# First expert stage of an attention, dense and routed-expert chain on one Trainium2 core: groups 2,3,3,3,3,2, an order planned with engine times, and part of the sums by accumulating transfers

## The chip, the core and the metric

The kernel runs on one core of one Trainium2 chip. Five engines work side by side, each through its own instruction list in order: PE (matrix multiplication), DVE and ACT (elementwise work), POOL and SP (here mainly issuers of transfers). Lists meet only at waits. The metric is device microseconds of the whole program.

## The reference

Four batches of 448 tokens pass through an attention, a dense layer pair and a routed layer pair:

```python
attn_out = _attn_ref(**attn_kwargs)          # (4, 12, 448, 64)
x = attn_out.transpose(0, 2, 1, 3).reshape(1792, 768)
h = x @ w_in                                 # (1792, 2048)
g = np.where(h > 0.0, h, np.exp(np.minimum(h, 0.0)) - 1.0)
x = g @ w_out                                # (1792, 768)
# then: argmax expert of x @ w_gate per token, relu(x @ w1[e]) @ w2[e], times the gate
```

The change touches the middle part, `h`, `g` and `g @ w_out`, called the first expert stage in its title. `w_in` and `w_out` arrive as doubles, read as pairs of 32-bit words, and are turned into floats on the chip ("decoding").

## The kernel before

All of the stage is in `moe1`. Products are made of two-part numbers: a value is split into a high part (an ACT copy to the matmul's type) and a low part (a DVE subtraction), in `hi_lo`. Each product takes three matmuls (high·high, high·low, low·high). Hidden units come in 16 blocks `f` of 128, tokens in four batches `b`. An "h unit" (`hmm`, L497) makes one `h[f, b]` in 18 matmuls of 448 columns. Its activation (`elu_act`, `elu_dve`) is three ACT steps (L511, L513, L514), two DVE steps (L522, L523), then the split (L470 on ACT, L471 on DVE). An "o unit" (`group_out`, L539) makes two of the six 128-row pieces `d` of `g @ w_out` for one batch, summed over the blocks of a group.

Batches 0 to 2 go first, group by group (`GROUPS`): all h units of a group, then its o units. Every piece of an o unit is taken from its PSUM bank by `group_evac`: the first group's is copied to `x2` (ACT L548, DVE L550), every later one is added to it by DVE (L552). Five banks (`acc0` to `acc4`) serve the pieces in turn; h units use two `h` banks and `acc5`. Blocks are decoded meanwhile (`Decoder.steps`): six steps, L138, L140 to L143 on DVE and L139 on ACT, then the row is split into `wi` or `wo` and stored to DRAM for the last batch. The blocks below `PRE` were decoded during the attention and are only loaded.

The order around it is written by a loop over units in `rest`. After each unit `background` spends a fixed budget on decoding and splitting (1.5 behind an h unit, 2.1 behind an o unit); a split is forced only when the unit that needs it is next. Two decoded rows at most wait (`len(held) < 2`, buffers `dec_p`). Loads and stores of rows stand on SP's list.

The last batch follows alone, block by block, with all weights loaded again. Between its units, and in the last group's o units, stand the routing steps of batches 0 to 2 (`route`).

The head of the stage overlaps the attention's end. `load_x` (L457) loads a batch's six tiles from DRAM into three `xraw` buffers, `split_x` splits them (L110, L112). The first two h units come between attention pieces; the tiles of batches 1 and 2 are split after the attention's last results (`p_av` L316, copied by L323, stored by L324).

## Time and profile before

| | us |
|---|---|
| median of 3 runs | 1301.95 |
| lowest, highest | 1298.39, 1317.82 |
| the profiled execution, its own time | 1304.9 |
| its span | 1303.1 |

In that execution PE is busy 1174.6 us (90%), DVE 793.1 (61%), ACT 661.6 (51%). The busy shares are means over stages with different limits, so the stretch of the stage is read by itself: when each phase begins, how many matmuls it holds, what PE waited for, and what clock was granted to it.

### The profile page before, as it was taken

The page shows a single profiled execution, that of the slowest core. Times are in us where ns is not written, and L with a number is a line of the kernel's source. Part 1 is how long each engine was busy: PE and PEld are TensorE (multiplying, and loading weights), DVE is VectorE, ACT ScalarE, POOL GpSimd, SP SyncE. Part 2 cuts the span into 40 slices and gives each one's busy share as a digit, 9 for nine tenths or more (in the row PEclk, how much of TensorE's full clock was granted, in tenths as well). Part 3 has the DMA queues.
Part 4 walks back from the last instruction along what each step waited for, and adds up shares of the span by engine and source line. Part 5 has one row for each costly group of instructions (what it writes and reads, how often), then busy time and mean ns, then how long its engine had stood idle before and what let it go on. Part 6 is the DMA issues. An engine that isn't in the chain of part 4 may idle for free.

```text
span 1303.1 us, 32292 instructions
## 1 busy us (share of the span) xinstructions
PE 1174.6 (90%) x13494; PEld 993.2 (76%) x13494; DVE 793.1 (61%) x1586; ACT 661.6 (51%) x1260; POOL 257.1 (20%) x424
## 2 busy tenths in 40 slices
PE   6889999899977996987969799888997999999996
PEld 2566566566666995977959698776897999999996
DVE  3777668667644746768577667344446555666663
ACT  3877778667754444152442433444444444455552
POOL 4756556556500000000000000000001101111110
PEclk7999999999988997998979899999997999999999
DMA  7787786776523422413223221333307747566661
GB/s 202 193 218 185 203 219 183 204 191 184 164 84 101 143 78 73 146 37 112 70 92 127 73 94 58 95 102 106 105 27 251 227 149 223 178 222 225 225 215 57
DMA packets 108991, 190.19 MB, mean 146 GB/s; under 512 B 44160, under 2 KB 68722, under 8 KB 108836
## 3 DMA queue, kind: packets, MB, share of 16 engines
q1 hardware_dynamic: 77284, 137.22, 33.6%
q0 software_dynamic: 31552, 50.82, 14.4%
q8 instruction: 108, 1.77, 0.6%
q14 instruction: 47, 0.39, 0.1%
HBM read 120.15 MB, written 30.09 MB: 115 GB/s over the span
## 4 chain that ended last, share of the span: by engine, by line
PE 72%; DVE 10%; ACT 9%; DMA 4%; issue 4%; POOL 0%; SPq 0%; POOLq 0%; ACTq 0%; DVEq 0%
PE p_o L539 12%; PE p_h L1106 11%; PE p_h L497 8%; PE p_z L1091 8%; PE p_post L281 6%; PE p_av L316 6%; PE p_pre L247 5%; PE p_qk L221 5%; PE acc L561 4%; PE p_y L1106 3%; DVE g L523 2%; DVE th L522 2%; DMA sp<-st 2%; ACT gh L470 2%; ACT th L513 2%
## 5 line engine op out<-in xcount | busy, mean ns | idle before, releaser
L238 POOL DMA_DIRECT2D sp<-st x360 | 207.8, 592 | 140.2 <-PE p_pre L247 72.2
L539 PE MATMUL p_o<-gh,woh 128*128 128x448 f32 x288 | 110.4, 383 | 43.0 <-ACT woh L470 34.2
L1053 POOL DMA_INDIRECT xg<-x2rows,tok x18 | 19.1, 1062 | 644.9 <-DMA x2rows<-rows 632.5
L258 ACT ACTIVATE pt<-p_pre,mx 128x448 f32<-128x448 f32 x180 | 112.5, 631 | 48.0 <-DVE mx L252 47.8
L281 PEld LDWEIGHTS p_post<-kp,pt 60*64 60x64 f32 (+1 forms) x5760 | 96.3, 134 | 50.4 <-ACT mt L291 31.3
L281 PE MATMUL p_post<-kp,pt 60*64 60x60 f32 (+1 forms) x5760 | 108.0, 220 | 15.1 <-issue 10.2
L252 DVE TENSOR_REDUCE mx<-p_pre 128x1 f32<-128x448 f32 x180 | 104.3, 619 | 28.1 <-PE p_pre L247 21.5
L291 ACT ACTIVATE mt<-p_post 128x960 f32<-128x960 f32 (+1 forms) x92 | 101.6, 1104 | 38.5 <-PE p_post L281 38.5
L497 PE MATMUL p_h<-xh,wih 128*128 128x448 f32 x288 | 109.8, 381 | 10.4 <-ACT wih L470 5.6
L522 DVE SCALAR_TENSOR_TENSOR th<-rm,th 128x448 f32<-128x448 f32 x64 | 40.0, 625 | 122.9 <-ACT rm L514 122.9
L1106 PE MATMUL p_h<-xgl,w1h 128*128 128x256 f32 (+1 forms) x384 | 110.0, 286 | 0.2 <-DVE xgl L1070 0.2
L1106 PE MATMUL p_h<-xgh,w1h 128*128 128x256 f32 (+1 forms) x384 | 110.1, 287 | 0.0
L221 PE MATMUL p_qk<-ks,qs 64*64 64x448 f32 x744 | 98.8, 561 | 12.6 <-issue 4.6
L1106 PE MATMUL p_h<-xgh,w1l 128*128 128x256 f32 (+1 forms) x384 | 109.8, 286 | 0.0
L539 PE MATMUL p_o<-gl,woh 128*128 128x448 f32 x288 | 108.8, 378 | 0.2 <-DVE gl L471 0.2
L539 PE MATMUL p_o<-gh,wol 128*128 128x448 f32 x288 | 108.8, 378 | 0.0
L497 PE MATMUL p_h<-xh,wil 128*128 128x448 f32 x288 | 108.1, 375 | 0.2 <-DVE wil L471 0.2
L497 PE MATMUL p_h<-xl,wih 128*128 128x448 f32 x288 | 107.7, 374 | 0.0
L316 PEld LDWEIGHTS p_av<-mt,vt 128*64 128x64 f32 x1536 | 78.0, 143 | 36.5 <-DVE kp L268 9.9
L247 PE MATMUL p_pre<-sp,kpre 60*64 60x448 f32 x720 | 101.3, 551 | 4.0 <-DMA sp<-st 4.0
L228 DVE COPY st<-p_qk 128x448 f32<-128x448 f32 x93 | 57.9, 623 | 73.0 <-PE p_qk L221 64.5
L539 PEld LDWEIGHTS p_o<-gh,woh 128*128 128x128 f32 x288 | 56.9, 197 | 51.0 <-ACT woh L470 35.3
(175 smaller groups left out, 2676.9 us busy)
## 6 DMA issues: line engine op xcount, KB each, us to landing
sp<-st POOLq DMA_DIRECT2D x352, 105.0 KB, 4.3
w1raw<-in_w_dram SPq DMA_DIRECT2D x64, 384.0 KB, 5.3
w2raw<-in_w_dram SPq DMA_DIRECT2D x48, 384.0 KB, 4.2
raw<-in_w_in_dram SPq DMA_DIRECT2D x13, 768.0 KB, 4.9
raw<-in_w_out_dram SPq DMA_DIRECT2D x13, 768.0 KB, 4.7
wtmp<-wscr SPq DMA_DIRECT2D x19, 384.0 KB, 3.2
wtmp<-oscr SPq DMA_DIRECT2D x19, 384.0 KB, 3.7
qs<-in_q_dram SPq DMA_DIRECT2D x32, 192.0 KB, 5.1
```

The lines of the kernel that those rows point to most:

```text
L221: mm(p[e][64 * a:64 * a + 64, :S], lhsT=qq[r, c:c + 64], rhs=kk[r], start=True, stop=True)
L238: nc.gpsimd.dma_start(t[64 * r:64 * r + 12 * T, c], st[cc][f:f + d * (T - 1) + 1:d])
L247: mm(ban[r][64 * c:64 * c + 64, :S], lhsT=kpre[x], rhs=t[x, c, :], start=True, stop=True)
L252: nc.vector.tensor_reduce(mxs[cc, g][:, r:r + 1], pre[cc, g][r][:, :S], AX.X, ALU.min)
L258: nc.scalar.activation(pt[cc, g][:, r], pre[cc, g][r][:, :S], AF.Exp, bias=mxs[cc, g][:, r:r + 1], scale=-1.0, accum_out=sms[cc, g][:, r:r ...
L281: mm(p[64 * (s % 2):64 * (s % 2) + 64, 2 * c + r, j * 12 * T:(j + 1) * 12 * T], lhsT=e[x, r, 64 * k0:64 * k0 + 64], rhs=kp[x, r].rearrange ...
L291: nc.scalar.activation(dst, src, AF.Copy)
L316: mm(p[64 * e:64 * e + 64, u, :n], lhsT=vt[cc // 4][:, j, h, :], rhs=mt[cc][:, j * H + h, :n], start=(j == 0), stop=(j == 3))
L497: mm(p[:, :S], lhsT=a[:, c], rhs=m, start=(i == 0), stop=(i == 17))
L539: mm(p[:, :S], lhsT=a[:, c], rhs=m, start=(k == 0), stop=(k == 3 * len(fs) - 1))
L1091: mm(zp[p][j, a][:, :384], lhsT=h2[h][:, i, c], rhs=w[:, a * 384:(a + 1) * 384], start=(i == 0 and m == 0), stop=(i == NFE - 1 and m == 2))
L1106: mm(q[:, :N], lhsT=a[:, kk, :], rhs=m[:, kk, :], start=(j == 0), stop=(j == len(seq) - 1))
```

## The change

Groups become 2,3,3,3,3,2 blocks; `PRE` stays 3. `background` now returns a planner: it keeps a running time for PE, ACT and DVE, adds a fixed cost for every step that is placed, and puts decoding and splitting steps one at a time into gaps of the plan (`fill_up`), between the steps of an activation too. The low part of an activation's split is placed late (`late`). `need` fixes the order of rows. Three decoded rows may wait instead of two. The sum of a piece goes to DVE as before, or to ACT (L572), which copies the bank to a tile `part` (four buffers, shared with `xraw`); POOL then issues a transfer that adds `part` to `x2` (L573). In the last group DVE takes all. The last group's units are interleaved (h of batches 0 and 1, o of 0, h of 2, o of 1 and 2), with up to two routing steps per o unit. At the head, batch 1 is loaded and split earlier and its first h unit stands ahead of the attention's last product. The activation writes in place (`th`, two buffers), and the rows of zeros that go to `x2rows` lie in the buffer of `rm`.

```diff
-GROUPS = [[0, 1, 2], [3, 4, 5], [6, 7, 8], [9, 10, 11], [12, 13], [14, 15]]
+GROUPS = [[0, 1], [2, 3, 4], [5, 6, 7], [8, 9, 10], [11, 12, 13], [14, 15]]
-PRE = len(GROUPS[0])
+PRE = 3
...
+    for b in (0, 1, None, 2, None, None):
+        if b is None:
+            units += [("o", len(GROUPS) - 1, outs, d) for d in range(0, KD, 2)]
+            outs += 1
+        else:
+            units += [("h", f, b) for f in GROUPS[-1]]
...
-        P["dec"] = Decoder(nc, sb, DM, 2, 1, 2)
+        P["dec"] = Decoder(nc, sb, DM, 2, 1, 3)
...
-            t = P["sb"].tile([128, S], F32, name="xraw", tag="xraw", bufs=3)
+            t = P["sb"].tile([128, S], F32, name="xraw", tag="xraw", bufs=4)
...
+        elif grouped:
+            to = wo[f] = pair(P["p1"], "wo", [128, DM], 4)
...
-    def group_evac(n, b, d):
+    def group_evac(n, b, d, dve):
...
+        elif dve:
+            nc.vector.tensor_tensor(x2[b][:, d, :], p, x2[b][:, d, :], ALU.add)
         else:
-            nc.vector.tensor_tensor(x2[b][:, d, :], p, x2[b][:, d, :], ALU.add)
+            t = P["sb"].tile([128, S], F32, name="part", tag="xraw", bufs=4)
+            nc.scalar.activation(t, p, AF.Copy)
+            nc.gpsimd.dma_start(x2[b][:, d, :], t, accum_op=ALU.add)
...
+        zrow = P["sb"].tile([128, S], F32, name="zrow", tag="rm")[:1]
...
+    need = []
+    for n, fs in enumerate(GROUPS):
+        need += [("in", f) for f in fs[:2] if n]
+        for i, f in enumerate(fs):
+            need += [("out", f)] + [("in", g) for g in fs[2 + i:3 + i]]
...
+        def put(e, ready, cost, fn):
+            T[e] = max(T[e], ready) + cost
+            fn()
+            return T[e] + .1
...
+                    raw[w, f] = P["dec"].load((w_in if w == "in" else w_out)[f]), max(T["dve"], T["act"]) + 6
...
+        DVE = {0: .6, 2: .6, 3: 1.0, 4: 1.0, 5: 1.0}
...
+                elif decs and decs[0] in raw and (len(started) < 3 or started[-3] in made):
+                    c.append((raw[decs[0]][1], .6, start))
...
+        def fill_up(e, until):
+            while True:
+                x = next_op(e)
+                if x is None or max(T[e], x[0]) + x[1] > until:
+                    return
+                x[2]()
...
             if v[0] == "o":
-                for d in (v[3], v[3] + 1):
-                    group_evac(v[1], v[2], d)
+                for i, d in enumerate((v[3], v[3] + 1)):
+                    at_end = end - (1 - i) * .61 * len(GROUPS[v[1]])
+                    fill_up("dve", at_end + .3)
+                    dve = n > last_n or T["dve"] < max(T["act"], at_end) + .1
+                    put("dve" if dve else "act", at_end, .65, lambda: group_evac(v[1], v[2], d, dve))
...
-                background(n, 1.5 if units[n][0] == "h" else 2.1)
...
+                relu, tanh, exp, w, sm, hi, lo = elu_steps(v[1:], place(i))
+                put("act", end, .6, relu)
+                put("act", end, .6, tanh)
+                e = put("act", end, .6, exp)
+                if late:
+                    put("dve", *late.pop())
+                fill_up("dve", e + .3)
+                fill_up("act", e + 1.1)
+                put("dve", e, .65, w)
+                e = put("dve", e, .65, sm)
+                late.append((put("act", e, .6, hi), .65, lo))
...
+    at(NSLOT + 1.5, 92, split_x, 1, range(3))
+    at(NSLOT + 1.5, 93, load_x, 1, range(3, 6))
+    at(NSLOT + 2, 94, split_x, 1, range(3, 6))
+    at(NSLOT + 2, 95, load_x, 2, range(4))
+    at(NSLOT + 2.2, 14, hmm, 0, 1, h_bank)
```

**First place: DVE, the step from a group's h units to its o units.** Before, at the end of the second group's h units (`wol` is the low part of a `w_out` row, `th`, `g` and `gl` belong to an activation, L138 to L143 decode, `x` is the sum):

```order
L141 SCALAR_TENSOR_TENSOR dec_m<-raw,dec_m 128x768
L142 SCALAR_TENSOR_TENSOR dec_p<-raw,dec_p 128x768
L143 SCALAR_TENSOR_TENSOR dec_p<-dec_m,dec_p 128x768
L471 TENSOR_TENSOR wol<-dec_p,woh 128x768
L522 SCALAR_TENSOR_TENSOR th<-rm,th 128x448
L523 SCALAR_TENSOR_TENSOR g<-p_o,th 128x448
L471 TENSOR_TENSOR gl<-g,gh 128x448
L138 TENSOR_SCALAR dec_p<-raw 128x768
L140 TENSOR_SCALAR dec_m<-raw 128x768
L141 SCALAR_TENSOR_TENSOR dec_m<-raw,dec_m 128x768
L552 TENSOR_TENSOR x_7732<-p_o,x_7732 128x448 x2
```

And in the changed kernel, at the same place of its second group (blocks 2, 3, 4):

```order
L143 SCALAR_TENSOR_TENSOR dec_p<-dec_m,dec_p 128x768
L536 SCALAR_TENSOR_TENSOR th<-rm,th 128x448
L537 SCALAR_TENSOR_TENSOR th<-p_h,th 128x448
L488 TENSOR_TENSOR gl<-th,gh 128x448
L488 TENSOR_TENSOR wol<-dec_p,woh 128x768
L536 SCALAR_TENSOR_TENSOR th<-rm,th 128x448
L537 SCALAR_TENSOR_TENSOR th<-p_h,th 128x448
L488 TENSOR_TENSOR gl<-th,gh 128x448
L138 TENSOR_SCALAR dec_p<-raw 128x768
```

The group's last `wol` has moved up: one activation (that of the ninth h unit) stands behind it before, two stand behind it now, and its decoding stands further ahead.

**Second place: ACT, the same group's o units.** Before (`part` doesn't exist, ACT takes no sums there):

```order
L470 ACTIVATE gh<-g 128x448
L139 ACTIVATE dec_p<-dec_p,ebias 128x768
L470 ACTIVATE wih<-dec_p 128x768
L139 ACTIVATE dec_p<-dec_p,ebias 128x768
L470 ACTIVATE wih<-dec_p 128x768
L139 ACTIVATE dec_p<-dec_p,ebias 128x768 x2
```

Now:

```order
L487 ACTIVATE gh<-th 128x448
L572 ACTIVATE part<-p_o 128x448 x5
L139 ACTIVATE dec_p<-dec_p,ebias 128x768
L487 ACTIVATE wih<-dec_p 128x768
L572 ACTIVATE part<-p_o 128x448 x2
L487 ACTIVATE wih<-dec_p 128x768
L139 ACTIVATE dec_p<-dec_p,ebias 128x768
L572 ACTIVATE part<-p_o 128x448 x2
L487 ACTIVATE woh<-dec_p 128x768
L139 ACTIVATE dec_p<-dec_p,ebias 128x768
L572 ACTIVATE part<-p_o 128x448 x3
```

Thirteen of the group's 18 pieces go through ACT and POOL (one more stands behind these rows), five in a row at its start; in the four groups after the first it is 13, 10, 13 and 10.

**Third place: SP, the loads at the head of the stage** (`xscr_61` and `xscr_62` hold batches 1 and 2, `xscr_63` takes the attention's last results). Before:

```order
L324 DMA xscr_63<-xc 128x2x88 x3
L478 DMA wtmp<-wscr_66 128x768
L478 DMA wtmp<-oscr_80 128x768
L457 DMA xraw<-xscr_61 128x448 x3
L457 DMA xraw<-xscr_62 128x448 x6
```

Now:

```order
L464 DMA xraw<-xscr_61 128x448 x6
L464 DMA xraw<-xscr_62 128x448 x4
L324 DMA xscr_63<-xc 128x2x88 x3
L464 DMA xraw<-xscr_62 128x448 x2
L495 DMA wtmp<-oscr_80 128x768
```

All of batch 1 and four tiles of batch 2 have moved ahead of the attention's last stores; two tiles of batch 2 still stand behind them.

## Rows read from the trace of the kernel before

**Rows 1.** The page's head.

```profile
span 1303.1 us, 32292 instructions
```

**Rows 2.** Stretches: length; busy PE, PEld, DVE, ACT, POOL (instructions); granted clock; DMA share, GB/s.

```profile
371.26:434.39 63.13, 50.29 (x355) 43.40 (x355) 28.75 (x50) 30.84 (x54) 0.00 (x0) 0.81 0.30 95
434.39:467.62 33.23, 33.10 (x164) 30.33 (x162) 24.38 (x39) 11.91 (x20) 0.00 (x0) 1.00 0.39 126
467.62:500.61 32.99, 32.99 (x163) 30.31 (x162) 17.90 (x27) 17.29 (x30) 0.00 (x0) 1.00 0.17 60
500.61:547.56 46.95, 35.55 (x163) 32.03 (x162) 36.49 (x55) 12.97 (x19) 0.00 (x0) 0.85 0.33 107
...
580.63:626.87 46.24, 34.82 (x164) 31.45 (x162) 36.39 (x55) 12.96 (x19) 0.00 (x0) 0.89 0.35 106
...
659.93:707.45 47.52, 36.13 (x164) 32.45 (x162) 36.30 (x55) 13.83 (x20) 0.00 (x0) 0.86 0.33 102
...
729.43:763.92 34.49, 25.61 (x109) 22.24 (x108) 27.87 (x44) 10.25 (x15) 0.00 (x0) 0.85 0.27 94
763.92:813.45 49.53, 48.95 (x256) 43.30 (x254) 29.76 (x64) 21.26 (x39) 0.00 (x0) 1.00 0.18 57
813.45:962.06 148.61, 132.86 (x665) 116.44 (x665) 65.96 (x140) 65.46 (x113) 0.00 (x0) 0.95 0.30 96
```

**Rows 3.** Who waited for whom on PE, 365 to 815 us.

```profile
PE p_o L539 <- ACT woh L470: 34.2, 3, 11.4
PE p_o L539 <- DVE x L552: 7.9, 2, 7.6
```

**Rows 4.** PE in order of time: start, us, line, operation, [idle before <-releaser].

```profile
386.29 6.68 PE L316 MATMUL p_av<-mt,vt 128*64 128x88 f32 x96 [3.47 <-ACT mt L291]
...
513.39 0.74 PE L539 MATMUL p_o<-gh,woh 128*128 128x448 f32 x1 [11.40 <-ACT woh L470]
...
515.30 0.57 PE L539 MATMUL p_o<-gl,woh 128*128 128x448 f32 x1
515.68 0.57 PE L539 MATMUL p_o<-gh,wol 128*128 128x448 f32 x1
```

**Rows 5.** DVE in order of time, ahead of the first long wait.

```profile
509.65 0.95 DVE L141 SCALAR_TENSOR_TENSOR dec_m<-raw,dec_m 128x768 f32<-128x768 uint32 x1
...
511.51 0.96 DVE L143 SCALAR_TENSOR_TENSOR dec_p<-dec_m,dec_p 128x768 f32<-128x768 f32 x1
```

**Rows 6.** Groups of instructions by shape, 434 to 764 us: busy, mean ns, idle before.

```profile
L552 DVE TENSOR_TENSOR x<-p_o,x 128x448 f32<-128x448 f32 x71 | 42.3, 619 | 9.4 <-PE p_o L539 9.2
L522 DVE SCALAR_TENSOR_TENSOR th<-rm,th 128x448 f32<-128x448 f32 x35 | 21.9, 624 | 49.5 <-ACT rm L514 49.5
L513 ACT ACTIVATE th<-rm 128x448 f32<-128x448 f32 x35 | 20.2, 578 | 1.1
L548 ACT ACTIVATE x<-p_o 128x448 f32<-128x448 f32 x9 | 4.6, 533 | 7.3 <-PE p_o L539 7.3
```

**Rows 7.** DMA queues: packets, MB, share of 16 engines; then issues: KB, us to landing.

```profile
q1 hardware_dynamic: 77284, 137.22, 33.6%
q0 software_dynamic: 31552, 50.82, 14.4%
...
sp<-st POOLq DMA_DIRECT2D x352, 105.0 KB, 4.3
...
raw<-in_w_in_dram SPq DMA_DIRECT2D x13, 768.0 KB, 4.9
...
xraw<-xscr SPq DMA_DIRECT2D x24, 224.0 KB, 3.0
```

**Rows 8.** ACT in order of time at the head.

```profile
386.14 1.50 ACT L110 ACTIVATE xh<-xraw 128x448 fp32r<-128x448 f32 x3
399.01 1.75 ACT L110 ACTIVATE xh<-xraw 128x448 fp32r<-128x448 f32 x3 [11.38 <-DMA xraw<-xscr]
```

**Rows 9.** Busy time by stretch, late in the program (columns as in group 2).

```profile
1193.00:1275.00 82.00, 82.00 (x607) 81.61 (x606) 51.35 (x77) 42.61 (x79) 14.69 (x16) 1.00 0.61 207
```

More of the change, by code (lines that the diff above doesn't have):

```diff
@@ L474, in scr, with load_row @@
         return (wscr if w == "in" else oscr)[f]
-    def load_row(w, f):
-        t = P["sb"].tile([128, 2 * DM], F32, name="wtmp", tag="raw", bufs=2)[:, :DM]
+    def load_row(w, f, t=None):
+        t = raw_tile()[:, :DM] if t is None else t
         nc.sync.dma_start(t, scr(w, f))
@@ L607, in row @@
             elif hf == 0:
-                T["row"] = P["sb"].tile([128, DM], F32, name="row", tag="dec_p", bufs=2)[:JC]
+                T["row"] = P["sb"].tile([128, DM], F32, name="row", tag="dec_p", bufs=3)[:JC]
             p = bank([JC, 3, 128], "tp")
@@ L814, in rest @@
         P["acc"] = pools.open("m_psacc", "right", PSUM)
-        need = sorted((where[w, f][0], w, f) for f in range(NF) for w in ("in", "out"))
-        need = [(w, f) for _, w, f in need if (w, f) not in (("in", 0), ("in", 1))]
-        loads, decs, splits = list(need), [k for k in need if k[1] >= PRE], list(need)
-        raw, cur, ready, held = {}, [], {k for k in need if k[1] < PRE}, set()
-        def free_after(w, f):
-            uses = where.get((w, f - (2 if w == "in" else 4)))
-            return uses[-1] if uses else -1
@@ L826, in load_next @@
-        def load_next():
-            if loads:
-                w, f = loads.pop(0)
-                if f < PRE:
-                    load_row(w, f)
-                else:
-                    raw[w, f] = P["dec"].load((w_in if w == "in" else w_out)[f])
-        def decode_step():
-            if not cur:
-                k = decs.pop(0)
-                held.add(k)
-                fns, dst = P["dec"].steps(raw.pop(k))
-                cur.extend([k, dst, fns])
-            k, dst, fns = cur
-            if len(fns) == 6:
-                for _ in range(3):
-                    fns.pop(0)()
-                return 1.1
-            fns.pop(0)()
-            if not fns:
-                rows32[k] = dst
-                ready.add(k)
-                cur.clear()
-                load_next()
-                nc.sync.dma_start(scr(*k), dst)
-            return .95
@@ L888, in weights @@
             load_pair(f + 3)
-        steps, banks, place = [], [0], {}
-        for n, u in enumerate(units):
-            if u[0] == "h":
-                g = [i for i, fs in enumerate(GROUPS) if u[1] in fs][0]
-                place[n] = sum(p[0] == "h" and p[1] in GROUPS[g] for p in units[:n])
-        ends = NU - KD // 2 * NG
-        load_next()
-        load_next()
-        for n in range(2, NU + 1):
-            if n == 2:
-                split_x(1, range(3))
-                load_x(1, range(3, 6))
-                split_x(1, range(3, 6))
+        steps, banks, late = [], [0], []
+        for n in range(3, NU + 1):
+            now = T["pe"]
             if n < NU:
@@ L905, in rest @@
                 if u[0] == "h":
+                    now = max(now, ready([("in", u[1])]))
                     hmm(u[1], u[2], h_bank if n % 3 < 2 else lambda: o_bank(5))
+                    T["pe"] = over[n] = now + 3.7
                 else:
+                    now = max(now, ready([("out", f) for f in GROUPS[u[1]]]))
                     for d in (u[3], u[3] + 1):
                         group_out(u[1], u[2], d, banks)
-            v = units[n - 1]
-            if v[0] == "o":
-                for d in (v[3], v[3] + 1):
-                    group_evac(v[1], v[2], d)
+                        if n >= last_n + 9 and steps:
+                            steps.pop(0)()
@@ new lines, in rest @@
+            if n < NU and late and units[n][0] == "o":
+                put("dve", *late.pop())
+            if n < NU:
+                for e in ("dve", "act", "dve"):
+                    fill_up(e, T["pe"] - (0 if e == "dve" else .5))
+            if n == 5:
+                fill()
+            if n == 20:
+                sel()
+            if 2 <= at_last < 2 + KD:
+                load_x(last_b, [at_last - 2])
+            if at_last == 6:
+                for f in range(2):
+                    load_row("in", f, P["sb"].tile([128, DM], F32, name="wtmp", tag="dec_p", bufs=3))
+                t = raw_tile()
+                for f in range(2):
+                    load_row("out", f, t[:, f * DM:(f + 1) * DM])
```

232 lines of the change are left out of this document (140 added, 92 removed).

## The prediction

> **What bounds it now.** I first read busy time by stretch, with bounds at the first matmul of each phase of the stage [rows 2]. The reader should see three kinds of stretch. An h phase of nine units, 162 matmuls, takes 32.99 us with PE busy throughout and the clock at 1.00, so 3.67 us a unit. The first group's o phase, also 162 matmuls, takes 33.23, or 0.205 us a matmul. The o phases of the next three groups hold the same 162 matmuls and take 46.95, 46.24 and 47.52, the fifth group's, of 108, takes 34.49, at granted clocks of 0.85 to 0.89. And the head, 63.13 us for nine h units, has a clock of 0.81.
>
> Then I read who PE waited for. In the o phases it was the high part of a `w_out` row, three times, 11.4 us at the longest, and once the sums on DVE, 7.6 of 7.9 us [rows 3]. The order of time shows the first of these: PE idles 11.40 us to 513.39, and afterwards matmuls start 0.38 us apart (515.30, 515.68) in place of 0.205, the lower of the two clock levels [rows 4]. On DVE the missing row's decoding steps end only with the one at 511.51, which lasts 0.96 [rows 5]. So PE sets the stage's time, and what it waits for is a decoding that DVE does late.
>
> DVE is late for two reasons. It is busy 17.90 of 32.99 us in an h phase but 36.49 in an o phase, which needs only 33.23 on PE [rows 2]: work is piled where there is no room. Over a whole group 54.4 of 66.2 would do.
>
> **Term 1, the stalls of groups two to five.** Against 33.23 (and 33.23·2/3 = 22.15 for two blocks) the four o phases lose 13.72 + 13.01 + 14.29 + 12.34 = 53.4 us [rows 2]; waits of 11.4, and 2 to 3 us of low clock behind each. In the changed order the group's last low part stands ahead of the last two activations of the h phase (first place), some 7 us before the first o unit, so the long wait has no source. The load moves too. Of each group's 18 sums ACT takes 13, 10, 13, 10, which frees DVE of 0.619 us each [rows 6]: 8.0 or 6.2 us, leaving 46 to 48 of 66.2. ACT gains 0.533 us a piece [rows 6], 6.9 us at most, on 17.29 + 12.97 = 30.3 [rows 2], so 37 of 66.2. Both fit with room, and the plan's fixed costs (0.6 for an activation step, 0.65 for DVE's) lie above the measured 0.578 and 0.624 [rows 6], so the order shouldn't drift late.
>
> In-order waits remain. ACT's decoding step stands behind five `part` copies, that is behind the sixth piece, 6·1.85 = 11 us into the o phase, and DVE's later decoding steps wait for it. This uses some 3 us of DVE's 18 us of slack per group. A late sum reaches PE only when five banks are full, five pieces or 9 us later. I leave 4 us for what slips through, with ends of 0 and 27 (half of the stalls).
>
> **Term 2, the new transfer.** Nothing in this trace accumulates. The nearest rows are a POOL transfer of 105 KB, 4.3 us from issue to landing, and a plain one of 224 KB, the size of `part`, 3.0 us [rows 7]. An accumulation also fetches the old values, so I bound it by 3.0 below and twice the slower row, 8.6, above, and take 5. It blocks in one place: four buffers, so the fifth `part` copy of a burst waits for the first transfer. Copies are 1.85 us apart, so a landing of up to 7 us isn't noticed there, and up to about 14 us the five banks cover it. Sustained, 13 pieces through four buffers need 13/4·(L + 0.5) us, which reaches 33.2 at L near 9.7. At 5 it costs nothing. The issues add nothing to ACT or SP, and POOL has no other work in the stage (0.00 in [rows 2]).
>
> Here is a rule that speaks against the change. By traffic, POOL's queue moved 50.82 MB in 14.4% of the span's 1303.1 us [rows 1, 7], 187.6 us of all 16 engines, so 0.85 us for one `part` and 11 us for 13; with the destination's values fetched the same way, 22. The loads already take 0.33 to 0.35 of such an o phase, about 16 us [rows 2]. Together 27 to 38 of 33.2 us: at the upper end 5 us too much per group. The Trainium skill, "Collectives: The Full Stack", section "The bandwidth ceiling: the fold count and why AG ≠ RS ≠ AR", says that an adding transfer is slower than a copy because it needs two source reads on the same ring; by that the upper end holds, and no run here shows it yet. I take the lower half, since the loads needed in an o phase can run on into the h phase, where DMA is used for 0.17 [rows 2].
>
> **Term 3, the head.** Before, PE waits for the attention's last rearranged tile, 3.47 us, then makes the last product in 6.68 [rows 4], and batch 1's later tiles come to ACT only at 399.01, after 11.38 us without work [rows 8]. Now batch 1's loads stand ahead of the stores (third place). ACT splits its first three tiles at 386.1 as before [rows 8]; the last two wait for a buffer and land 3.0 us later [rows 7], at 390. So the first h unit of batch 1 fills the wait and ends near 393, the attention's product then takes 5 to 6.7, to 398.5, and the next h unit ends at 402. There a new wait begins. The third-next h unit needs the bank of batch 1's first, and that activation stands on ACT behind batch 2's splits; two of those need loads that SP issues behind the attention's last stores, near 399, so they land at 402.3 and are split by 403.6. Three ACT and two DVE steps [rows 6] give 406.7. One unit at low clock, 3.67 + 2.3, and one at full clock end at 416.4, when the first o unit begins. The zeros now lie in `rm`: an activation waits for their store, which I cost at 1.5 us of late sums. The head then loses (416.4 + 1.5 - 371.26) - 6·3.67 = 24.6 us against 63.13 - 9·3.67 = 30.1 [rows 2], a gain of 5.5, with ends of 0 and 13.
>
> **Term 4, the last group and the last batch.** 49.53 + 148.61 us [rows 2]. The same matmuls and routing steps are there in another order: five more routing steps go with the last group, five fewer with the last batch. All are PE work in both places, and the waits between an activation and a rank step stay. I cost it at 0, ±5. Regrouping itself moves no matmul, 864 + 864 either way.
>
> **Sum.** 53.4 - 4 + 5.5 = 54.9 us. The profiled execution took 1304.9, with 1.8 around its span of 1303.1 [rows 1], so 1250.0 for one like it. It lies 2.95 above the median of 1301.95, so I predict 1247 us.
>
> **Rivals.**
> A. *The queues collide.* DMA overflows by 5 us in each of four o phases, decoded rows come late, and DVE stands at a load with sums behind it. Against it: loads are due 6 us after issue in the plan and take 4.9 [rows 7], and banks cover 9 us. It gives back 20 us: 1267, and with half of the stalls 1274.
> B. *The adding transfers are slow, and the kernel gets slower.* ACT blocks at the buffer wait, PE at the banks. 46 pieces through four buffers take 11.5·(L + 0.5) us where PE needs 133. The gain of 59 is gone at 192 us, L = 16; at L = 18.5 the kernel is 2% slower, about 1328. For it: no row shows such a transfer. Against it: 3.0 and 4.3 us [rows 7], a quarter of that.
> C. *The order doesn't hold.* Engines reach planned steps late by the in-order waits above, and long waits return under another name, as DVE or ACT sums in front of PE. Most of term 1 comes back: 1290.
> D. *Everything overlaps.* No residue, the head gains 13, the last batch 5: 1231.
>
> **How the numbers follow.** The forecast, 1238 to 1262, has a chance of 0.66: its steps rest on PE's measured rate, and PE kept its clock at 1.00 over 82 us of unbroken work late in the program [rows 9], so long work without stalls costs no clock. A has 0.15 (1262 to 1282), B 0.06, C 0.08, D 0.05. The range 1236 to 1280 leaves out nearly all of D, B, C and the end of A, 0.2. Faster or slower by over 2%, about what a measurement of this kernel tells from no change, means below 1276 or above 1328: faster 0.84 (the forecast, D, most of A), within 2% 0.11 (the rest of A, C, part of B), slower 0.05.
>
> **What would show it.** Right: the o phases of blocks 2 to 13 near 33 us at a clock near 1.00, no wait on `woh` there, DVE near 47 us a group. Term 2: landings of `x<-part` under 7 us, and ACT's waits before `part` ended by PE, not by DMA. Rival A: DVE waits before its first decoding step ended by the raw loads in the o phases. Rival B: ACT's `part` copies ended by DMA, and PE waiting for ACT's sums. Term 3: the first o matmul near 416, a PE wait near 402 ended by DVE. It would be wrong if a stall of several us stood in every group.

## The result, and the profile after

The changed kernel takes 1236.11 us, median of three (1233.28 to 1244.87); against the kernel before the ratio is 0.948, 95% interval 0.934 to 0.962. In a later comparison of six and eleven runs it was 0.944 (0.942 to 0.947), 1237.93 against 1311.27. So the change is faster, as forecast, but by more: the prediction was 1247 with a range from 1236, and 0.948 of 1301.95 is 1234.2, just below that range (0.944 of it would be 1229).

The stretches of the changed kernel, cut at the first matmul of each phase as in [rows 2] and with the same columns: the head, the first group's o phase, then h and o phases in turn, the last group, the last batch.

```profile
373.52:415.93 42.41, 34.48 (x300) 29.81 (x301) 20.51 (x39) 22.42 (x40) 0.00 (x0) 0.84 0.32 92
415.93:438.44 22.51, 22.22 (x110) 20.12 (x108) 17.18 (x26) 11.69 (x20) 0.00 (x0) 1.00 0.48 148
438.44:471.53 33.09, 33.09 (x164) 30.40 (x163) 25.14 (x41) 22.32 (x38) 0.00 (x0) 1.00 0.33 108
471.53:504.39 32.86, 32.86 (x163) 30.42 (x162) 25.21 (x35) 15.61 (x26) 11.31 (x13) 1.00 0.85 214
504.39:537.18 32.79, 32.79 (x163) 30.41 (x162) 22.58 (x34) 21.59 (x37) 0.14 (x1) 1.00 0.31 94
537.18:570.05 32.87, 32.87 (x164) 30.42 (x162) 24.27 (x34) 13.21 (x22) 8.59 (x10) 1.00 0.74 177
...
668.49:701.35 32.86, 32.86 (x163) 30.42 (x162) 23.79 (x33) 13.64 (x22) 8.60 (x10) 1.00 0.63 148
701.35:756.95 55.60, 50.70 (x268) 44.02 (x267) 32.31 (x74) 22.74 (x42) 0.13 (x1) 1.00 0.30 86
756.95:891.57 134.62, 126.18 (x654) 111.24 (x652) 63.64 (x132) 63.88 (x110) 0.00 (x0) 0.99 0.33 105
```

The reader should see that an o phase now takes what an h phase takes, 32.86 against 46 to 48 us [rows 2], at a clock of 1.00, and that DVE is as busy in one as in the other (25.14 and 25.21, against 17.90 and 36.49). The waits of PE between the first o matmul and the last group are down to a single row, where [rows 3] had 34.2 and 7.9:

```profile
PE p_o L556 <- ACT x L567: 0.3, 1, 0.3
```

Where the 69.0 us between the two spans (1303.1 and 1234.1) come from:

| stretch | before | after | gain |
|---|---|---|---|
| start to the first h matmul (attention, not edited) | 371.26 | 373.52 | -2.3 |
| head: loss against 3.67 us a unit | 30.1 | 20.4 | 9.7 |
| the rest, to the start of the last group | | | 55.1 |
| last group, and last batch to its last product | 208.94 | 201.03 | 7.9 |
| from there to the end | 330.2 | 331.7 | -1.5 |

The third line is what remains of 64.8 us (392.66 from the first h matmul to the last group before, 327.83 after) without the head's 9.7. In the fourth, the stretch is counted up to the last output product, 10.8 us beyond the bound of [rows 2]. The head is compared by its loss because it holds nine h units before and six after.

One execution is no fine measure of the whole. The attention's code is the same in all kernels below, and the first h matmul came anywhere between 367.55 and 377.60 us. So I read each experiment from its own stretches, and from the total only where it was repeated.

### The profile page after: what moved, and what is told of

Its sections match the earlier page's. It is cut to its first block, busy times and chain, and to the rows that moved or that the text cites. A ratio compares the mean times of both kernels' runs of the same rounds, so it can differ in the third digit from the quotient of the medians.

```text
span 1234.1 us, 32461 instructions
## 1 busy us (share of the span) xinstructions
PE 1153.3 (93%) x13494; PEld 979.1 (79%) x13494; DVE 766.9 (62%) x1538; ACT 684.5 (55%) x1308; POOL 298.0 (24%) x470
## 3 DMA queue, kind: packets, MB, share of 16 engines
q1 hardware_dynamic: 77284, 137.22, 35.8%
q0 software_dynamic: 38176, 61.37, 20.5%
## 4 chain that ended last, share of the span: by engine, by line
PE 84%; ACT 5%; DMA 4%; DVE 4%; issue 3%; POOL 1%; SPq 0%; ACTq 0%; POOLq 0%; DVEq 0%
PE p_h L516 14%; PE p_o L556 13%; PE p_h L1191 11%; PE p_z L1176 8%; PE p_post L281 7%; PE p_av L316 6%; PE p_pre L247 5%; PE p_qk L221 5%; PE p_o L516 4%; PE acc L582 4%; PE p_y L1191 3%; DMA sp<-st 2%; PE p_t L90 1%; ACT mt L291 1%; DVE th L536 1%
## 5 line engine op out<-in xcount | busy, mean ns | idle before, releaser
L252 DVE TENSOR_REDUCE mx<-p_pre 128x1 f32<-128x448 f32 x180 | 104.0, 618 | 28.8 <-PE p_pre L247 22.9
L573 POOL DMA_DIRECT2D x<-part x46 | 41.0, 912 | 304.3 <-ACT part L572 299.8
L556 PE MATMUL p_o<-gh,woh 128*128 128x448 f32 x288 | 106.6, 370 | 2.8 <-DVE x L569 2.5
L556 PE MATMUL p_o<-gl,woh 128*128 128x448 f32 x288 | 105.1, 365 | 0.0
L556 PE MATMUL p_o<-gh,wol 128*128 128x448 f32 x288 | 105.0, 364 | 0.0
L316 PEld LDWEIGHTS p_av<-mt,vt 128*64 128x64 f32 x1536 | 74.2, 137 | 33.5 <-DVE kp L268 11.3
L112 DVE TENSOR_TENSOR w2l<-w2raw,w2h 128x768 fp32r<-128x768 f32 (+1 forms) x60 | 60.7, 1012 | 51.7 <-ACT w2h L110 51.7
L316 PE MATMUL p_av<-mt,vt 128*64 128x120 f32 (+1 forms) x1536 | 84.1, 263 | 1.6 <-issue 1.1
L516 PE MATMUL p_h<-xh,wih 128*128 128x448 f32 x204 | 77.5, 380 | 8.6 <-DVE th L537 7.2
L1227 POOL DMA_INDIRECT out_dram<-yrow,put x18 | 23.9, 1325 | 252.9 <-ACT w1h L110 86.9
```

The source lines that it names most:

```text
L252: nc.vector.tensor_reduce(mxs[cc, g][:, r:r + 1], pre[cc, g][r][:, :S], AX.X, ALU.min)
L316: mm(p[64 * e:64 * e + 64, u, :n], lhsT=vt[cc // 4][:, j, h, :], rhs=mt[cc][:, j * H + h, :n], start=(j == 0), stop=(j == 3))
L516: mm(p[:, :S], lhsT=a[:, c], rhs=m, start=(i == 0), stop=(i == 17))
L556: mm(p[:, :S], lhsT=a[:, c], rhs=m, start=(k == 0), stop=(k == 3 * len(fs) - 1))
```

## Experiments

### Is it the order, or the relief of DVE?

Two runs, each with one half of the change. The first keeps the plan and takes the transfers out:

```diff
-dve = n > last_n or T["dve"] < max(T["act"], at_end) + .1
+dve = v[1] > 0 or T["dve"] < max(T["act"], at_end) + .1
```

> All sums of groups two to six on DVE, no accumulating transfer; planner, groups and head as in the changed kernel. Theory 1 (the order alone removes the stalls): DVE then carries 54 of 66 us a group, which fits if it is spread, so the three full o phases take 33 to 35 us each, the stretch from the first o matmul to the last group stays within 295 us (285.4 in the changed kernel), total 1236 to 1246. Theory 2 (the relief of DVE is needed): the o phases take 38 us or more each, with PE waiting for a row of w_out or for a sum on DVE; the stretch takes 305 us or more, total 1256 or more.

Its four o phases (same columns):

```profile
471.56:504.43 32.87, 32.87 (x164) 30.43 (x163) 26.36 (x40) 8.51 (x12) 0.00 (x0) 1.00 0.33 108
537.22:574.61 37.39, 34.79 (x164) 31.39 (x163) 33.23 (x49) 9.17 (x13) 0.00 (x0) 0.95 0.41 133
607.40:640.26 32.86, 32.86 (x164) 30.42 (x162) 26.36 (x40) 8.50 (x12) 0.00 (x0) 1.00 0.33 108
673.05:710.75 37.70, 34.78 (x163) 31.46 (x162) 33.24 (x49) 10.03 (x14) 0.00 (x0) 0.95 0.31 106
```

What PE and ACT waited for there, from 438.77 to 710.75 us (in all, times, longest):

```profile
PE p_o L556 <- ACT woh L487: 5.2, 2, 2.6
...
ACT wih L487 <- DVE dec_p L143: 52.8, 8, 9.7
```

Two phases have no stall at all without a single transfer; in the other two DVE works 33.23 us, ACT waits for its decoding, and PE waits again for a row of `w_out`, 2.6 us each. The stretch from the first o matmul to the last group is 294.5 us, inside theory 1's bound, against 285.4; the total, 1248.43, lies a little above it. So the order alone (the plan with its groups and buffers) brings 46 of the 55.1 us and the transfers 9.1, by one execution of each.

The second is the kernel before with the transfers alone (48 of the 72 sums of groups two to five; the expectation's 66 is a slip):

```diff
-        else:
+        elif n == len(GROUPS) - 1 or d % 3 == 0:
             nc.vector.tensor_tensor(x2[b][:, d, :], p, x2[b][:, d, :], ALU.add)
+        else:
+            t = P["sb"].tile([128, S], F32, name="part", tag="xraw", bufs=3)
+            nc.scalar.activation(t, p, AF.Copy)
+            nc.gpsimd.dma_start(x2[b][:, d, :], t, accum_op=ALU.add)
```

> The kernel before, with two of every three sums of groups two to five sent by ACT and an accumulating transfer (48 of 66), nothing else changed. DVE is relieved of 12 x 0.62 = 7.4 us in an o phase, 36.5 to 29 of 33.2. Theory 1 (the order is what counts): the long wait for a row of w_out stays, since its decoding still comes after the h phase; the four o phases lose 30 to 50 us (53.4 before), total 1275 to 1300. Theory 2 (DVE's load in the o phase is what counts): it now fits, the phases lose 15 or less, total 1255 to 1268.

Two of its o phases, then PE's waits from 500 to 770 us:

```profile
507.51:554.22 46.71, 35.31 (x164) 31.82 (x162) 30.80 (x44) 18.38 (x30) 9.60 (x11) 0.85 0.63 153
587.29:633.42 46.13, 34.71 (x164) 31.37 (x162) 30.83 (x44) 18.27 (x30) 9.66 (x11) 0.89 0.64 157
```

```profile
PE p_o L539 <- ACT woh L470: 34.2, 3, 11.4
PE p_o L539 <- DVE x L552: 7.6, 1, 7.6
```

DVE's busy time in the o phase falls from 36.49 to 30.80, less than PE needs, and the phase stays at 46.71; the waits are those of [rows 3] to a tenth. The four phases together take 1.1 us less than before (174.1 and 175.2): they lose 52.3 us, a little more than theory 1 allowed and far from theory 2. The total, outside both ranges, was 1313.71 against 1304.52, which the stage doesn't explain: from its first h matmul to its last product it takes 600.4 us, 601.6 before; the attention ended 6.3 us later and the tail was 3.6 longer. So in the kernel before it was not DVE's load that stalled PE: the row that is begun too late stalls it at 36.49 us of DVE work and at 30.80 alike. In that order the relief is worth 1.1 us, and with the plan 9.1.

### The third row under way, and the groups

```diff
-elif decs and decs[0] in raw and (len(started) < 3 or started[-3] in made):
+elif decs and decs[0] in raw and (len(started) < 2 or started[-2] in made):
```

> The plan may have only two decoded rows under way, not three (the third buffer is there, but no row is begun in it). Theory 1 (the stalls went because rows are placed by time, two in flight do): o phases within 1 us of 32.9, total 1234 to 1240. Theory 2 (the third row gives the lead): a wait for a row of w_out of 3 us or more returns in most groups, o phases 36 us or more, total 1250 or more.

The o phases took 34.11, 33.84, 33.84 and 33.84 us, the total 1239.85: 1.0 us a group, no long wait, and 3.9 us from the first o matmul to the last group (289.3 for 285.4). The third row is a small part of the order's gain, though not quite nothing as theory 1 had it. Its head took 40.30 us, 2.1 less, with nearly the same idle time of PE (8.2 and 7.9 us) and at a granted clock of 0.92 in place of 0.84, so that I put it down to the clock and not to the edit. Then the groups of before, with all else as in the changed kernel:

```diff
-GROUPS = [[0, 1], [2, 3, 4], [5, 6, 7], [8, 9, 10], [11, 12, 13], [14, 15]]
+GROUPS = [[0, 1, 2], [3, 4, 5], [6, 7, 8], [9, 10, 11], [12, 13], [14, 15]]
```

> Groups 3,3,3,3,2,2 as before, all else as in the changed kernel. Theory 1 (regrouping moves no matmul and the plan holds either way): the time from the first h matmul to the end of the last batch is within 4 us of the changed kernel's 518.1, total 1233 to 1241. Theory 2 (the short first group is part of the gain, by fewer h units at the low clock or by a lead for the decoding): 6 us or more longer, with stalls in the first group or the first o phase.

Its head and first o phase:

```profile
367.55:420.44 52.89, 44.54 (x355) 38.90 (x355) 27.05 (x49) 29.89 (x53) 0.00 (x0) 0.90 0.29 85
420.44:454.08 33.64, 33.49 (x164) 30.32 (x163) 27.60 (x39) 16.02 (x26) 0.00 (x0) 1.00 0.59 188
```

From the first h matmul to the last group it takes 327.6 us (327.8), to the last product 532.0 (528.9), in all 1233.23. This is theory 1: the regrouping is worth nothing that one run shows, and the head's loss is the same without the short first group: 52.89 - 9·3.67 = 19.9 us.

### What the accumulating transfer costs

In the changed kernel, the line of the transfers (POOL's time to issue one, in ns, and us to landing):

```profile
L573 POOL DMA_DIRECT2D x<-part x46: 860/869/1256, 476.2 to 700.6; - x46
...
DMA to landing us min/median/max: 3.2/6.0/10.0
```

What ACT waited for ahead of `part`, 438 to 701 us:

```profile
ACT part L572 <- PE p_o L556: 47.6, 22, 3.1
...
ACT part L572 <- DMA x<-part: 3.3, 2, 1.8
```

Then all 72 sums by transfer, in place of 46:

```diff
-dve = n > last_n or T["dve"] < max(T["act"], at_end) + .1
+dve = n > last_n or (v[1] == 0 and T["dve"] < max(T["act"], at_end) + .1)
```

> All 72 sums of groups two to five go by ACT and an accumulating transfer (46 before). An accumulation added 1.42 us of all 16 DMA engines in the changed kernel. Theory 1 (transfers have room, only the four buffers bound): 18 pieces through four buffers need 18/4 x (6.0 + 0.5) = 29 us of 33, the o phases take 33 to 36 us and the whole 1236 to 1248. Theory 2 (the changed kernel is at the edge of the DMA engines): 18 x 1.42 + 16 = 42 us of transfers in 33, landings grow past 10 us, ACT's copies wait for them, the o phases take 38 to 45 us, total 1256 to 1285.

An o phase, and the h phase that lost most:

```profile
472.83:505.70 32.87, 32.87 (x163) 30.43 (x162) 24.25 (x32) 16.81 (x28) 13.56 (x15) 1.00 0.87 224
...
572.98:612.62 39.64, 35.01 (x163) 31.97 (x162) 22.61 (x34) 22.91 (x40) 4.30 (x5) 0.91 0.39 100
```

The waits of PE and ACT between the first o matmul and the last group:

```profile
PE p_h L516 <- DVE th L537: 8.4, 3, 4.6
...
ACT part L572 <- DMA x<-part: 60.9, 41, 3.8
```

Both theories missed the place. The o phases stay at 32.87 with DMA busy for 0.87, even below what theory 1 allowed, but ACT now stands 41 times at the transfers, 60.9 us in all, as theory 2 has it. What it leaves undone is missing in the next h phase, where PE waits for an activation: three h phases take 34.4, 39.6 and 35.8 us in place of 32.8. The stretch is 11.9 us longer, the total 1258.90, in theory 2's range. With 46 transfers the kernel is close to this edge, not over it.

### The head

Batch 1's loads, splits and first h unit put back behind the attention's last product, as a block at the start of `rest` (the same five steps; the lines that put them there are left out):

```diff
-    at(NSLOT + 1.5, 92, split_x, 1, range(3))
-    at(NSLOT + 1.5, 93, load_x, 1, range(3, 6))
-    at(NSLOT + 2, 94, split_x, 1, range(3, 6))
-    at(NSLOT + 2, 95, load_x, 2, range(4))
-    at(NSLOT + 2.2, 14, hmm, 0, 1, h_bank)
```

> Only the head is put back: loads and splits of batch 1 and its first h unit behind the attention's last product. Theory 1 (the head's gain is this order): the first o matmul comes 6 to 10 us later than the changed kernel's 415.9, the loss over six h units at full rate is 26 to 30 us (20.4), total 1241 to 1247. Theory 2 (the gain comes from the short first group or the planner): the first o matmul within 2 us of 415.9.

The head took 45.75 us in place of 42.41 (42.73 in the changed kernel run again), the total was 1241.21: 3.0 to 3.3 us, half of what theory 1 expected, of the 9.7. Eight executions of the changed head, e3's aside, took 41.9 to 43.6 us, so this is 2 to 4 us; PE's idle time is 1.0 us of it (8.93 and 7.93), the rest matmuls at a lower clock (0.81 and 0.84). For the rest I looked for a loss in the head of the kernel before that the plan removes. There is one that the prediction had passed over, the third row of `w_in` (waits of PE before, 371.26 to 434.39):

```profile
PE p_h L497 <- ACT wih L470: 5.6, 2, 4.6
```

So, in the kernel before, that row's split ahead of the activation of the unit before it:

```diff
             elif n > 2:
+                if n == 5:
+                    background(n, 1.5)
                 elu(v[1:], place[n - 1])
...
-            if n < ends:
+            if n < ends and n != 5:
                 background(n, 1.5 if units[n][0] == "h" else 2.1)
```

> The kernel before with the split of the third w_in row put ahead of the activation of the unit before it. Theory 1 (the 4.59 us wait at 420.6 and the low clock behind it are the part of the head's loss that the prediction did not count): the wait falls to 2 us or less and the head from 63.1 to 57 to 60 us. Theory 2 (the activations pushed back take its place): a wait on th or g of 3 us or more appears, the head within 1.5 us of 63.1.

Its head and its first o phase:

```profile
368.14:425.53 57.39, 47.78 (x355) 41.46 (x356) 26.56 (x46) 27.99 (x49) 0.00 (x0) 0.85 0.26 79
425.53:465.22 39.69, 35.12 (x164) 31.55 (x163) 26.76 (x44) 14.68 (x24) 0.00 (x0) 0.96 0.46 160
```

PE's longest wait in that o phase, in the order of time:

```profile
439.88 0.47 PE L539 MATMUL p_o<-gh,woh 128*128 128x448 f32 x1 [4.38 <-ACT x L548]
```

The head is 5.7 us shorter, as theory 1 says, and the first o phase 6.5 longer, 39.69 against 33.23: ACT, an activation in arrears, is late with a sum, and it stands 1.56 us of that at a row that DVE has not decoded yet. From the first h matmul to the last group nothing is gained (392.8 and 392.7; the total, 1303.57, says no more). So the wait was the sign of arrears on ACT, not their cause. With the plan, and these same groups, neither stretch shows it (52.89 and 33.64 above): in that head PE waits 8.8 us in place of 13.7, of these the waits for the high part of a `w_in` row fall from 5.6 to 0.5 us and all others together are 8.1 and 8.3. Of the 10.2 us that this head is shorter, 4.5 are idle time of PE and 5.7 are matmuls at a higher clock (0.90 for 0.81). That the plan spreads ACT's work between 400 and 440 us is my reading, and no run separates it from the fourth `xraw` buffer.

The same again in the changed kernel, whose h-bank wait came as forecast, where ACT stands at the two late tiles of batch 2 (PE in the order of time):

```profile
394.98 3.86 PE L316 MATMUL p_av<-mt,vt 128*64 128x88 f32 x96
407.01 0.45 PE L516 MATMUL p_h<-xh,wih 128*128 128x448 f32 x1 [4.32 <-DVE th L537]
```

```diff
-        for ks in (range(4), range(4, 6)):
-            split_x(2, ks)
-            if ks[0] == 0:
-                load_x(2, range(4, 6))
+        split_x(2, range(4))
+        load_x(2, range(4, 6))
...
+            if n == 3:
+                split_x(2, range(4, 6))
```

> The changed kernel with the splits of batch 2's last two tiles put behind the activation of the first unit of batch 1. Theory 1 (the 4.32 us bank wait at 407 is ACT standing at those two late loads): that wait falls under 1 us and the head from 42.4 to 36 to 39 us, total 4 to 6 us less. Theory 2 (the loads themselves land late): the wait moves to the first product of batch 2, the head within 1.5 us of 42.4.

Its head and its first o phase:

```profile
375.66:412.04 36.38, 32.74 (x300) 28.21 (x301) 19.47 (x37) 21.79 (x39) 0.00 (x0) 0.86 0.31 93
412.04:437.32 25.28, 22.64 (x109) 20.11 (x108) 18.14 (x28) 12.02 (x21) 0.00 (x0) 1.00 0.50 152
```

The bank wait is gone and the head takes 36.38 us, 6.3 less than in the changed kernel run again, as theory 1 says; the first o phase takes 25.28 instead of 22.55, with 1.8 us of PE's wait for a sum on ACT. Net 3.5 us by the last group, and in the total nothing that shows, against theory 1's 4 to 6 us: 1239.42 (four runs) against 1237.93 (six).

### The last group and the last batch

The gain of 7.9 us here was not forecast. Two runs undid one difference each: the routing step ahead of the activation in two units of three, and fewer steps in the last group.

```diff
                 hmm(f, last_b, h_bank)
+                if f < NF - 1 and f % 3 < 2 and steps:
+                    steps.pop(0)()
                 elu((f, last_b))
```

> In the last batch a routing step stands again ahead of the activation in two units of three, as before the change. Theory 1 (the last batch gained because the activation goes first): PE's waits for g, for the rows of routing and for th come back, the last batch takes 139 to 146 us instead of 134.6, total 1239 to 1248. Theory 2 (it gained by carrying fewer routing steps): it stays within 1.5 us of 134.6.

```diff
-                        if n >= last_n + 9 and steps:
+                        if n >= last_n + 9 and steps and popped[0] < 8:
+                            popped[0] += 1
                             steps.pop(0)()
```

> The last group takes 8 routing steps instead of 12, and the last batch 4 more. Theory 1 (a routing step costs PE the same in both places): last group 52 to 54 us (55.6), last batch 136.5 to 138.5 (134.6), their sum within 1.5 us of 190.2. Theory 2 (steps cost less in the last group, where no activation waits behind them): the sum grows by 3 to 8 us.

The two stretches together, to the last product, took 206.4 and 205.6 us, the totals were 1245.93 and 1240.76. But eight executions whose code here is the changed kernel's (its two profiles, and those of the runs above with this part unedited) took 201.0, 201.5, 204.0, 204.2, 204.2, 204.4, 205.7 and 205.9, mean 203.9. Neither run stands out, and the 134.6 and 190.2 of the expectations were those of the shortest of the eight, so both are inconclusive. Before, it was 208.9, and 208.3 and 210.2 in the two runs that left this part of the kernel before alone. The gain is thus about 5 us, and the rest of the 7.9 is a good execution: luck, as far as the change goes.

The largest difference between PE's waits is one for `r_tot`, a sum on DVE over the experts picked, which the rank product reads. Before, PE waited for it twice; after, of three rank products the first waited for nothing, the one at 790.97 0.33 us and the one at 850.81 4.29. Other waits changed too and nearly cancel: those for ACT's `row` (4.2 us before) are gone, those for `r_lm` (2.4) and for sums in the last group (1.0 to 2.5) are new. In all PE idles 16.7 us before and 12.2 after in six of the eight executions, and the waits for `r_tot` are 3.3 of these 4.5 us. The waits of PE before, 763.92 to 972.86:

```profile
PE rp L664 <- DVE r_tot L661: 7.9, 2, 4.0
```

In the changed kernel, PE's second rank product of the last batch:

```profile
850.81 0.36 PE L685 MATMUL rp<-r_tot,c_tri 112*112 112x8 f32 x2 [4.29 <-DVE r_tot L682]
```

and DVE ahead of it, in the order of time:

```profile
848.09 0.62 DVE L536 SCALAR_TENSOR_TENSOR th<-rm,th 128x448 f32<-128x448 f32 x1 [2.54 <-ACT rm L535]
848.75 0.62 DVE L537 SCALAR_TENSOR_TENSOR th<-p_h,th 128x448 f32<-128x448 f32 x1
850.01 0.62 DVE L488 TENSOR_TENSOR gl<-th,gh 128x448 fp32r<-128x448 f32 x1 [0.64 <-ACT gh L487]
850.55 0.20 DVE L682 TENSOR_REDUCE r_tot<-r_oh 112x8 f32<-112x32 f32 x1
```

`r_tot`, 0.20 us of work, stands on DVE behind the whole activation of the unit just ahead. Where the step is issued behind the output product instead, DVE has the same work in front of `r_tot`, but PE has 18 matmuls to do first, some 3.8 us, and the wait shrinks by about that, 4.29 to 0.33. Steps fall behind an activation and behind an output product in turn, so an odd shift exchanges the two. One step fewer in the last group makes such a shift:

```diff
-                        if n >= last_n + 9 and steps:
+                        if n >= last_n + 9 and steps and popped[0] < 11:
+                            popped[0] += 1
                             steps.pop(0)()
```

> The changed kernel with 11 routing steps in the last group instead of 12, so that every later step moves by one place. Theory 1 (the place decides: a rank product issued behind an activation waits, one issued behind an output product does not): batch 1's rank product, 0.33 us of wait in the changed kernel, now stands behind an activation and waits 4 us, batch 2's, 4.29 us, now waits under 1. Theory 2 (it is how far DVE is behind in that part of the batch): batch 2's still waits 4 us, batch 1's under 1.

PE's two rank products of the last batch:

```profile
802.49 0.54 PE L685 MATMUL rp<-r_tot,c_tri 112*112 112x8 f32 x2 [4.30 <-DVE r_tot L682]
...
860.39 0.36 PE L685 MATMUL rp<-r_tot,c_tri 112*112 112x8 f32 x2 [0.33 <-DVE r_tot L682]
```

The two waits change places, 0.33 and 4.29 become 4.30 and 0.33: theory 1 (the total, 1240.43, is that of the changed kernel). What such a wait is worth was tried in the kernel before, with `r_tot` made three steps earlier:

```diff
 def pick():
     ...
     nc.vector.tensor_tensor(oh, cst["em8"][:JC], ix.to_broadcast(sh), ALU.is_equal)
+    tot = small("tot", [JC, NE])
+    nc.vector.tensor_reduce(tot, oh.rearrange("p t e -> p e t"), AX.X, ALU.add)
 def rank():
-    oh, ones = T["oh"], cst["ones"]
-    tot = small("tot", [JC, NE])
-    nc.vector.tensor_reduce(tot, oh.rearrange("p t e -> p e t"), AX.X, ALU.add)
+    oh, ones, tot = T["oh"], cst["ones"], T["tot"]
```

> The kernel before with r_tot computed in the step that picks the expert, nothing else. Theory 1 (the rank waits and the low clock behind them are what the last group and last batch had to give): both waits of 3.97 us vanish and the stretch from the last group's start to the last product falls from 208.9 to 193 to 200 us, as in the changed kernel with the same edit (195.8), total 9 to 15 us less than before. Theory 2 (the order of activation and routing step has its own share): the waits vanish but the stretch stays at 202 to 206 us.

Its last group, and its last batch to the last product:

```profile
763.71:813.24 49.53, 48.95 (x255) 43.29 (x254) 29.82 (x64) 21.26 (x39) 0.00 (x0) 1.00 0.17 57
813.24:961.33 148.09, 138.71 (x727) 121.53 (x727) 69.09 (x145) 69.38 (x120) 0.00 (x0) 0.99 0.29 96
```

Both waits vanish and the sum is 197.6 us, 11.3 less than 208.9; the total is 0.9918 of before (0.989 to 0.995, nine and twelve runs), 10.7 us. So a wait of 3.97 us cost 5.7: of the 11.3 us, 6.7 were PE's idle time and 4.6 were matmuls that ran at the low clock. One such wait less is about the 5 us that the changed kernel gained here. The order of activation and step need not have a share: with the same edit in the changed kernel (below) the stretch takes 195.8 and 200.1 us, so with no rank wait in either kernel these executions leave no difference between them. One execution each cannot exclude one or two us.

### A faster version

The same edit in the changed kernel:

> The changed kernel with the sum r_tot computed in the step that picks the expert, three routing steps ahead of the rank product that waits for it. Theory 1 (each wait of that product is DVE's backlog ahead of r_tot): PE's waits for r_tot fall from 4.6 us to under 1, total 3 to 6 us less than the changed kernel. Theory 2 (the wait moves to the next operation that needs the same DVE work): the wait returns under another name, total within 2 us.

and with it the head's edit from above, and the zeros in a buffer of `th`:

```diff
-name="zrow", tag="rm")[:1]
+name="zrow", tag="th", bufs=2)[:1]
```

> Both of the edits above, and the zeros in a buffer of th in place of rm. If the gains add: 7 to 12 us less than the changed kernel, 1224 to 1232. If the clock or the tail gives part of it back: 2 to 6 us less.

The last group, and the last batch to its last product, of the two:

```profile
697.96:893.74 195.78, 185.98 (x982) 163.13 (x980) 99.34 (x210) 90.73 (x159) 0.14 (x1) 1.00 0.30 97
698.20:898.29 200.09, 191.72 (x982) 168.01 (x980) 99.46 (x210) 90.71 (x159) 0.13 (x1) 0.97 0.30 94
```

In neither does PE wait for `r_tot`, and only 0.6 us for one `row` is new, so the wait did not come back under another name: theory 1. All four were compared on one chip with the kernel before at 1311.27 us:

> The changed kernel again, beside the next three: total 1233 to 1245; first h matmul to first o matmul 42 to 43.5 us; last group and last batch to the end of the last product 201 to 206 us. Both theories of the next runs are read against this one.

| kernel | median us (runs) | ratio to before | 95% |
|---|---|---|---|
| changed kernel again | 1237.93 (6) | 0.9442 | 0.9415 to 0.9469 |
| late tiles behind the activation | 1239.42 (4) | 0.9454 | 0.9414 to 0.9493 |
| rank sum early | 1229.22 (4) | 0.9398 | 0.9367 to 0.9430 |
| both | 1228.50 (6) | 0.9367 | 0.9336 to 0.9399 |

The changed kernel came as expected (head 42.73, last group and batch 204.0 us). Both edits together beat it: 9.4 us by the medians, inside the 7 to 12 expected, and the intervals don't overlap. Nearly all of it is the rank sum (8.7 by its median, more than the 3 to 6 expected, though its interval overlaps the changed kernel's); what the head's edit adds can't be told from nothing.

## Why the prediction was right, and where it failed

Three terms were low, by 5.7, 4.2 and 7.9 us; attention and tail took back 2.3 and 1.5. With these the forecast sum of 54.9 becomes the 69.0 of the two profiles. Terms 1 and 3 had the mechanism right and the size too small; the step that failed in its mechanism is in term 4.

**Term 1** was right in its cause, and its size was 5.7 us short (49.4 forecast, 55.1 measured). Order and relief were argued together; apart, the order is worth 46 us, the relief 9.1 behind it and 1.1 without it. DVE took 46.5 to 50.4 us a group for the 47 forecast. The 4 us left for in-order waits were not lost: those waits exist (ACT's `woh` behind DVE's decoding, 7.7 us in five) but end before PE needs the row. This residue of 4 us, which measured nothing, is the larger part of the miss. Another 1.7 us came from PE's pace, most of it in the o phases: 32.87 us for 162 matmuls that took 33.23 [rows 2]. One reading was loose: in the fifth group PE stood 7.6 us at a sum on DVE [rows 3], not at a row, and the low clock behind the four stalls cost 1.6 to 3.5 us, not 2 to 3. That sum's wait is also gone with the plan, and stays in the run with transfers alone.

**Term 2** was right: cost 0, landing 6.0 us for an estimate of 5, ACT waiting for PE's pieces (47.6 us) and hardly for the transfers (3.3). The traffic came out between the two bounds, 0.85 and 1.7 us for one piece. POOL's queue took 20.5% of 1234.1 us, 253.0, and 187.6 before [rows 1, 7], so by estimate one accumulation costs 65.4/46 = 1.42 us of all 16 engines; against the run with the plan and no transfers (15.3% of 1246.6 us, 190.7) it is 1.35. The Trainium skill, "Collectives: The Full Stack", section "The bandwidth ceiling: the fold count and why AG ≠ RS ≠ AR", says of the reduce step of a collective that its add needs two source reads where a copy needs one; the trace agrees in direction, at 1.6 to 1.7 times a copy. An o phase's DMA share rose to 0.85, and PE lost nothing by it; that loads due there ran on into the h phases, as the prediction argued, fits their DMA share of 0.31 to 0.36, where three of four had 0.17 to 0.19. DVE waited 2.5 us in all for raw loads. Rival A's collision came when 26 more transfers were added, and then in the h phases: DVE's waits for the raw loads that it named rose to 10.1 us, but what PE waited for were activations.

**Term 3** was right in its sequence and 4.2 us too low (9.7, not 5.5). Counted from the first h matmul, the bank wait ends at 33.5 us where 35.4 was forecast, since the attention's product took 3.86 us instead of 5 to 6.7: behind an h unit, the clock was 1.00 from 395 to 402 us. The zeros in `rm`, priced at 1.5, held PE up nowhere (ACT waited 2.11 us for their store), and the last two units took 0.8 less. Batch 1's first unit did not quite fill the wait: PE still stood 3.5 us in front of it, and it ended 21.5 us after the first h matmul where 21.7 was forecast. As an account of the gain the step was incomplete: the order of batch 1 brings 3.0 to 3.3 of the 9.7, and the wait for the third row of `w_in`, which the prediction didn't name, stood for arrears of ACT that the plan clears.

**Term 4** failed: 0 forecast, 7.9 us in the two profiles, about 5 over the eight executions. "The waits between an activation and a rank step stay" is the step. They depend on which place a step lands in, and with another count of steps one rank product came to the place where PE has other work first: the waits for `r_tot` went from 7.9 us to 4.6, and such a wait, with the low clock behind it, is worth 5.7. I had costed steps by their work and the waits by their number. The ±5 around it should have had the two waits in it, and the lower end of the range with them.

**Rivals.** B and C did not occur: landings of 3.2 to 10.0 us, no long wait under another name. D, everything overlaps, at 1231, was the nearest, and it got the smallest chance, 0.05. I had charged each unknown (residue, zeros, rank waits) with a loss or with nothing and hardly any with a gain, so the range was short below.

What stays open: how the head's remaining 6 us or so divide between the plan and the fourth buffer, and whether the order of activation and step in the last batch is worth one or two us.

## What to carry to other kernels

When an engine is both overloaded in a phase and late in it, try order and relief apart: here relief alone brought 1.1 us, and order alone five sixths of 55.1. A short operation that another engine waits for belongs in the step where its input is ready; where it stands one step later, its wait is set by whatever the step count happens to put in front of it. After a wait is removed, read the next stretch as well as its own: in three runs here (the third row, the late tiles, all sums by transfer) the engine's arrears appeared one phase later.

## What was not expected of the hardware

- An accumulating transfer of 224 KB into on-chip memory landed after 3.2, 6.0 and 10.0 us (least, median, most), kept POOL for 0.87 us to issue, and took by estimate 1.42 us of all 16 DMA engines with 46 of them and 1.39 with 72 (22.9% of 1257.0 us, less 187.6); with the 190.7 us of the run without transfers taken off instead, it is 1.35 both times.
- The granted clock after the same wait was not always the same. In the last group PE waits 2.40 us for `r_lm` in each of the eight executions of the same code; the group then took 55.60 and 55.62 us at a clock of 1.00 in two of them, and 56.8 to 58.1 at 0.91 to 0.94 in the other six. The changed kernel, and the changed kernel run again, where matmuls take 0.57 us from 744.22 on:

```profile
743.04 0.51 PE L90 MATMUL tp<-c_ident,x 128*112 128x128 f32 x3 [2.40 <-DVE r_lm L662]
745.08 0.36 PE L556 MATMUL p_o<-gl,woh 128*128 128x448 f32 x1
```

```profile
742.36 0.51 PE L90 MATMUL tp<-c_ident,x 128*112 128x128 f32 x3 [2.41 <-DVE r_lm L662]
744.59 0.57 PE L556 MATMUL p_o<-gl,woh 128*128 128x448 f32 x1
```

- Time that the edits cannot reach varies more than several of the effects studied: the first h matmul came within a span of 10 us (367.55 to 377.60).
